# Set attention and a tanh-residual MLP on one core: weights decoded on VectorE alone, another split of the product's read-out, whole rows of natural x, a wider row pitch and a new written order

## The chip, the cores and the metric

One core of one Trainium2 chip runs the kernel. The metric is the device time of one execution in microseconds (us). The kernel before was timed in three runs: 218.50, 219.16 and 217.11 us, median 218.5. The profile shown was taken in a further execution of 216.84 us, in which the span from the first to the last instruction is 215.1 us.

## The reference

For each of 4 batches, 32 inducing vectors I attend to x (12480 rows of 128), which gives h (32 x 128); then every row of x attends to h. The result goes through an MLP without bias:

```python
def mab(q, kv):
    s = scale * (q @ kv.transpose(0, 2, 1))
    s = s - s.max(-1, keepdims=True)
    a = np.exp(s)
    a /= a.sum(-1, keepdims=True) + 1e-09
    return a @ kv
h = mab(I, x)
y = mab(x, h)
h2 = y @ w_in                       # 128 -> 2048
return ((h2 - np.tanh(h2)) @ w_out) # 2048 -> 128
```

All is fp32, except that the two weight matrices come as 64-bit floats, which the kernel turns to fp32 itself. Since y is a weighted mean of the 32 rows of h, the kernel does not run the MLP on 49920 rows: it runs a tangent form of it once per batch on the 32 rows of h ("feed", which gives a 32 x 128 table P) and then only weighs P for each row. A check at the end (lines 611 to 673) decides on the chip whether that is exact enough; the general path behind it does not run here.

## The kernel before, in words

x is cut into 4 batches of 8 steps of 1536 rows, and a remainder of 192 rows per batch. Each step's x is loaded once, transposed (channels on partitions), as a tile of 128 x 1536 (768 KB); 16 such tiles are kept. A step takes part twice.

First pass, per step: four score matmuls of x with the inducing vectors (line 311), VectorE copies them to SBUF with their running maximum (line 365). After a group of 3, 3 or 2 steps the four quarter maxima on partitions 0, 32, 64 and 96 are joined into one (lines 376 to 380), ScalarE takes the exponential of the group (line 385), VectorE transposes it in 32 x 32 blocks (line 410), and TensorE multiplies it with x in its natural layout (lines 417 and 426). Natural x comes in one of two ways: loaded from memory for 11 of 32 steps (line 392, written as 12 pieces of 512 bytes per partition, since each piece has a column of ones behind it), or by 12 transposes on TensorE, which ScalarE copies out (lines 404 and 407). When a batch's 8 steps are through, "feed" makes h and P (lines 450 to 544).

Second pass, per step: four score matmuls with the centred h (line 311 again), VectorE takes the maximum (line 552), ScalarE the exponential (554) and a weight w (556), GpSimd multiplies P with w (560), and TensorE multiplies both: 12 matmuls of 129 columns into 4 banks, the "product" (568). There is one set of 4 banks for it, so the next product waits until this one has been read. VectorE adds 1e-9 to the 12 sums and takes their reciprocals (584, 585) and scales banks 0 and 1 (588); ScalarE copies banks 2 and 3 (590), GpSimd scales these in SBUF (592); the step is then stored (603).

Each 512-column piece of a weight matrix (8 pieces) is loaded into an output tile `ot` and decoded by nine instructions on three engines: low half and mantissa on ScalarE (270, 289), bit fields on VectorE (273, 276, 284), exponent clamp, sum and scale on GpSimd (280, 281, 292, 295).

The order on every engine is that of one list: each operation has an assumed cost and a rank (a table of numbers by kind, batch and step), a list scheduler plays them through, and the instructions are issued in the order of the starts that it gives. All DMAs are issued from SyncE's queue (SP), in order: one that waits for a tile to come free holds the ones behind it.

Of the kernel before, what the change touches and what calls it, by code (L numbers as in the profile page):

```python
# [23 lines left out]
PITCH = 1536  # L24
# [5 lines left out]

POLY = (0.333333333, -0.133333309, 0.0539675967, -0.0218625754, 0.00882625035,
        -0.0034783865, 0.00124215751, -0.000337689816, 4.84671135e-05)

# [4 lines left out]

RANK = {
    "ind": [(-746.3, 138.31)],  # L40
    "load r": [(-1052.2, 40.15)],
    "r": [(-79.7, 170.53)],
    "load w": [(-698.6, 25.14)],
    "w": [(197.5, 163.77)],
    "guard": [(1549.9, 28.69)],
# [775 lines left out]
```

## Time and profile before

| what | value |
|---|---|
| median of three runs | 218.5 us (217.11 to 219.16) |
| the profiled execution: time, span | 216.84 us, 215.1 us |
| busy: TensorE, VectorE, ScalarE, GpSimd | 165.6, 155.1, 114.1, 120.3 us |
| DMA moved | 64.49 MB, 300 GB/s over the span |
| mean granted TensorE clock | 0.947 |

Busy times are sums over the whole span; no engine is busy for all of it. The DMA share of a stretch is the mean busy share of the 16 DMA engines; GB/s divided by that share is the rate while they are busy. A chain of waits lists the pieces of work that followed one another without slack, to the last instruction.

### The profile page before, as it was taken

The numbers are of one execution on the slowest core, as the hardware profiler recorded it, in microseconds if no ns is written. First come the engines' busy times: TensorE is split into PE (matmuls) and PEld (weight loads), VectorE is DVE, ScalarE is ACT, GpSimd is POOL, SyncE is SP. The second block draws the span as 40 slices with busy tenths as digits, with TensorE's granted clock in tenths as the row PEclk, the third lists the DMA queues.
The fourth block names the chain that finished last, engine by engine and source line by source line (L and its number), as shares of the span: only waits on it lengthen the run. The fifth ranks groups of instructions, "written<-read, shape, count | busy, mean of one in ns | idle before, by whom it ended". The sixth has DMA issues, their size and how long they took to land.

```text
span 215.1 us, 6700 instructions
## 1 busy us (share of the span) xinstructions
PE 165.6 (77%) x2632; PEld 103.1 (48%) x2632; DVE 155.1 (72%) x484; ACT 114.1 (53%) x223; POOL 120.3 (56%) x151
## 2 busy tenths in 40 slices
PE   2295489968799599997998799979999877634420
PEld 2163245735365276553746466546665472324310
DVE  3376979979896588895957678878679888774420
ACT  3557655758556166727537286355674535552210
POOL 2498997999204444543354166333476467877650
PEclk9999999999999999999999999999999999985555
DMA  6989975999879979999999999999455645586571
GB/s 187 365 358 365 379 274 164 348 419 420 237 249 350 362 276 384 326 397 365 374 343 348 367 332 381 356 329 351 141 218 226 252 190 240 221 330 241 207 259 66
DMA packets 27879, 64.49 MB, mean 300 GB/s; under 512 B 1504, under 2 KB 18400, under 8 KB 27840
## 3 DMA queue, kind: packets, MB, share of 16 engines
q1 hardware_dynamic: 27840, 63.99, 81.5%
q8 instruction: 23, 0.38, 0.7%
q14 instruction: 16, 0.13, 0.2%
HBM read 38.42 MB, written 25.56 MB: 298 GB/s over the span
## 4 chain that ended last, share of the span: by engine, by line
PE 31%; DMA 24%; DVE 16%; POOL 14%; issue 8%; ACT 3%; SPq 0%; POOLq 0%; ACTq 0%; DVEq 0%
DMA x<-in_xT 10%; DMA out<-ot 10%; PE PS L568 10%; PE PS L311 9%; POOL ot L280 7%; DVE ot L588 4%; PE PS L404 4%; PE PS L417 4%; DMA ot<-in_w_in 3%; POOL ot L592 3%; DVE ot L284 2%; ACT ot L590 2%; POOL ot L281 2%; POOL win_sb L292 1%; PE PS L524 1%
## 5 line engine op out<-in xcount | busy, mean ns | idle before, releaser
L592 POOL TENSOR_TENSOR ot<-ot,r 128x384 f32<-128x384 f32 (+1 forms) x66 | 53.1, 821 | 52.8 <-ACT ot L590 29.4
L407 ACT COPY xn<-PS 128x512 f32<-128x512 f32 x63 | 35.1, 587 | 18.6 <-PE PS L404 16.5
L568 PE MATMUL PS<-pw,e 32*128 32x129 f32 (+1 forms) x784 | 33.9, 304 | 13.6 <-DVE ot L588 10.9
L404 PE MATMUL PS<-ident,x 128*128 128x128 f32 x252 | 39.2, 290 | 5.5 <-DVE s L365 5.5
L568 PEld LDWEIGHTS PS<-pw,e 32*128 32x128 f32 (+1 forms) x784 | 27.5, 200 | 27.3 <-POOL ot L592 12.6
L590 ACT COPY ot<-PS 128x768 f32<-128x768 f32 (+1 forms) x33 | 26.0, 789 | 27.0 <-DMA out<-ot 11.3
L404 PEld LDWEIGHTS PS<-ident,x 128*128 128x128 f32 x252 | 27.9, 145 | 24.3 <-DVE s L365 7.2
L311 PE MATMUL PS<-x,ind_sb 128*32 128x384 f32 x256 | 27.4, 506 | 9.1 <-DMA x<-in_xT 6.3
L588 DVE TENSOR_TENSOR ot<-PS,r 128x768 f32<-128x768 f32 (+1 forms) x33 | 31.2, 945 | 3.5 <-DMA out<-ot 2.7
L560 POOL TENSOR_SCALAR pw<-P,w 128x129 f32<-128x129 f32 (+1 forms) x36 | 21.9, 612 | 17.2 <-ACT P L530 5.1
L311 PE MATMUL PS<-x,hC 128*32 128x384 f32 x256 | 26.4, 494 | 3.8 <-ACT e L554 2.3
L554 ACT ACTIVATE e<-PS,negm 128x384 f32<-128x384 f32 (+1 forms) x33 | 19.0, 577 | 17.8 <-PE PS L568 8.9
L417 PE MATMUL PS<-xn,et 128*32 128x129 f32 x672 | 24.1, 276 | 0.0
L280 POOL TENSOR_SCALAR ot<-ot 128x512 uint32<-128x512 uint32 x8 | 16.7, 2084 | 8.2 <-DVE ot L276 7.4
L417 PEld LDWEIGHTS PS<-xn,et 128*32 128x32 f32 x672 | 17.5, 109 | 5.9 <-issue 5.2
L365 DVE TENSOR_SCALAR_CACHE_REDUCE s<-PS 128x384 f32<-128x384 f32 x32 | 17.3, 548 | 4.1 <-PE PS L311 3.9
L552 DVE TENSOR_REDUCE negm<-PS 128x1 f32<-128x384 f32 (+1 forms) x33 | 17.7, 543 | 3.5 <-PE PS L311 3.3
L584 DVE TENSOR_SCALAR r<-PS 128x12 f32<-128x12 f32 (+1 forms) x33 | 5.6, 170 | 20.2 <-PE PS L568 14.4
L284 DVE SCALAR_TENSOR_TENSOR ot<-ot 128x512 uint32<-128x512 uint32 x8 | 12.9, 1612 | 7.1 <-POOL ot L281 7.0
L385 ACT ACTIVATE s<-s,nb 128x1152 f32<-128x1152 f32 (+1 forms) x12 | 13.8, 1152 | 7.3 <-DVE nb L380 7.2
L410 DVE STREAM_TRANSPOSE et<-s 128x384 f32<-128x384 f32 x32 | 16.9, 553 | 0.9 <-ACT xn L407 0.4
L311 PEld LDWEIGHTS PS<-x,ind_sb 128*32 128x32 f32 x256 | 6.0, 109 | 15.7 <-issue 5.1
(121 smaller groups left out, 183.7 us busy)
## 6 DMA issues: line engine op xcount, KB each, us to landing
x<-in_xT SPq DMA_DIRECT2D x32, 768.0 KB, 7.7
out<-ot SPq DMA_DIRECT2D x32, 768.0 KB, 4.8
xn<-in_xn SPq DMA_DIRECT2D x11, 768.0 KB, 7.5
ot<-in_w_in SPq DMA_DIRECT2D x4, 512.0 KB, 7.7
ot<-in_w_out SPq DMA_DIRECT2D x4, 512.0 KB, 4.0
xR<-in_xR SPq DMA_DIRECT2D x1, 384.0 KB, 3.0
outR<-ot SPq DMA_DIRECT2D x1, 384.0 KB, 5.0
ind_sb<-in_indT SPq DMA_DIRECT2D x1, 16.0 KB, 2.8
```

The costliest lines, as they stand in the source:

```text
L280: nc.gpsimd.tensor_scalar(out=e(), in0=e(), scalar1=896.0, scalar2=1151.0, op0=ALU.max, op1=ALU.min)
L311: nc.tensor.matmul(ps[q * m:(q + 1) * m, :n], lhsT=w(q) if callable(w) else w, rhs=row, start=True, stop=True)
L404: nc.tensor.transpose(out=ps.get()[:, j * 128:(j + 1) * 128], in_=x.get()[:, (4 * h + j) * 128:(4 * h + j + 1) * 128], identity=ident)
L407: add("ACT", 0.68, lambda ps=ps, xn=xn, h=h: nc.scalar.copy(out=xn.get()[:, 4 * h:4 * h + 4, 0:128], in_=ps.get().rearrange("p (j c) -> p ...
L417: nc.tensor.matmul(hacc.get()[q * m:(q + 1) * m, g * 130:g * 130 + 129], lhsT=et.get()[:, j, :], rhs=xn.get()[:, j, 0:129], start=(k == 0 ...
L552: add("DVE", 0.1 + T / 850, lambda: nc.vector.tensor_reduce(out=mcol, in_=ps.get()[:, :T], axis=AX.X, op=ALU.max, negate=True), reads=[ps] ...
L554: add("ACT", 0.2 + T / 1300, lambda: nc.scalar.activation(out=e2.get()[:, :T], in_=ps.get()[:, :T], func=AF.Exp, bias=mcol), reads=[ps, st ...
L560: nc.gpsimd.tensor_scalar(out=pw.get()[p, 0:129], in0=t[p, 0:129], scalar1=w.t[p], scalar2=None, op0=ALU.mult)
L568: nc.tensor.matmul(o.get()[:BL, q, k * 129:(k + 1) * 129], lhsT=e2.get()[p, k * BL:(k + 1) * BL], rhs=pw.get()[p, 0:129], start=True, stop ...
L588: add("DVE", 0.1 + 2 * T / 870, lambda: nc.vector.tensor_tensor(out=res(0, 2), in0=ov(0, 2)[:, :, :, :128], in1=wide(0, 2), op=ALU.mult), ...
L590: add("ACT", 0.2 + 2 * T / 1300, lambda: nc.scalar.copy(out=res(2, 4), in_=ov(2, 4)[:, :, :, :128]), reads=[o, ot], writes=[c], pri=("o", ...
L592: add("POOL", 0.1 + T / 500, lambda q=q: nc.gpsimd.tensor_tensor(out=res(q, q + 1).rearrange("p q k c -> p (q k) c"), in0=res(q, q + 1).re ...
```

## The change

Seven parts come together.

1. **Weights.** The nine instructions of a piece become seven on VectorE, four with one input and three with two; ScalarE and GpSimd have none. The pieces are loaded into x tiles and no longer into output tiles.
2. **Product's read-out.** VectorE takes the reciprocals of its own two banks' sums (6 per partition) straight from PSUM, ScalarE copies the sums of its two banks to SBUF, where VectorE takes their reciprocals later. The 1e-9 is put into P's column of ones. P times w moves from GpSimd to ScalarE.
3. **Last batch.** Steps 1, 3, 5 and 7 of the last batch write their product into a second set of four banks (those of the other PSUM tiles); its exponentials and outputs go into tiles that are done with.
4. **Group maxima.** The quarters are brought together by 4 GpSimd copies, one VectorE reduction, and 4 copies back, in place of 8 VectorE reductions.
5. **Natural x.** 13 steps, not 11, are loaded, as whole rows of 6336 bytes with the ones in them.
6. **Row pitch** of xT and out: 1696 in place of 1536 elements; 1536 of them are moved.
7. **Order.** The scheduler and its ranks give way to a fixed list of operation numbers. Some small matmuls of "feed" are cut into 32-column pieces, and small operations of its check move to ScalarE and GpSimd.

```diff
-PITCH = 1536
+PITCH = 1696
+ORDER = [int(n) for n in """
+1 2 3 69 0 77 4 73 21 70 74 80 75 72 71 92 76 22 94 23 83 78 95 24 93 25 90 81 26 91 29 27 82 28 37 84 79 101 85 117
...
-            buf = at("ot")
+            buf = at("x")
...
-            add("ACT", 0.7, low, reads=[buf], writes=[outs[k], lo_b], pri=p)
-            add("DVE", 0.65, bits, reads=[buf], writes=[lo_b], pri=p)
-            add("ACT", 0.65, mantissa, reads=[buf], writes=[lo_b], pri=p)
-            add("DVE", 0.65, shift, reads=[buf], writes=[e_b], pri=p)
-            add("POOL", 1.4, clamp, reads=[buf], writes=[e_b], pri=p)
-            add("DVE", 0.9, sign, reads=[buf], writes=[e_b], pri=p)
-            add("POOL", 1.4, join, reads=[buf, lo_b], writes=[outs[k]], pri=p)
-            add("POOL", 1.4, scale, reads=[buf, e_b], writes=[outs[k]], pri=p)
+            add("DVE", 0.34, magnitude, writes=[buf], pri=p, lock=True)
+            add("DVE", 0.3, clamp, writes=[buf], pri=p, lock=True)
+            add("DVE", 0.3, fields, writes=[buf], pri=p, lock=True)
+            add("DVE", 0.6, high, writes=[buf, outs[k]], pri=p, lock=True)
+            add("DVE", 0.3, power, reads=[outs[k]], writes=[buf], pri=p, lock=True)
+            add("DVE", 0.6, low, writes=[buf], pri=p, lock=True)
+            add("DVE", 0.6, join, reads=[buf], writes=[outs[k]], pri=p, lock=True)
...
+                for q in range(NQ):
+                    nc.gpsimd.tensor_copy(mq.t[:, q, :], mx.t[q * m:(q + 1) * m, :nm])
...
-        add("POOL", 0.35 * len(P4s), weigh, reads=[w, *(P4_b if len(P4s) > 1 else [P4_b[n // NS]])], writes=[pw], pri=("s2", b, s))
-        o = at("o")
+        add("ACT", 0.29, lambda: nc.scalar.activation(out=pw.get()[:, 0:129], in_=P4s, func=AF.Copy, scale=w.get()),
+            reads=[w, P_b], writes=[pw], pri=("s2", b, s))
+        o = at("o2" if last and s in SECOND else "o")
...
-            nc.vector.tensor_scalar(out=rs.t[:BL], in0=ov(0, NQ)[:, :, :, 128], scalar1=1e-9, scalar2=None, op0=ALU.add)
-            nc.vector.reciprocal(out=rs.t[:BL], in_=rs.t[:BL])
+        add("DVE", 0.05 + 0.016 * nv * nb, lambda: recip(*sums(0, nv)), reads=[o, rs], writes=[ra], pri=("o", b, s))
+        add("ACT", 0.1, lambda: nc.scalar.copy(out=sums(nv, NQ)[1], in_=sums(nv, NQ)[0]), reads=[o, rs], writes=[rc], pri=("o", b, s))
...
-        "xn": np.ascontiguousarray(np.stack([xs[b, s].reshape(KB, 128, C).transpose(1, 0, 2) for b, s in sorted(LOADED)])),
+        "xn": np.stack([np.pad(xs[b, s].reshape(KB, 128, C).transpose(1, 0, 2), ((0, 0), (0, 0), (0, 4)), constant_values=1.0)
+                        for b, s in sorted(LOADED)]),
```

Three places show how the instructions move. GpSimd's queue at the start, behind its memsets (`ot` an output tile with a raw weight piece, `mx` the maxima of a group, `nb` their joined negative). Before:

```order
L280 TENSOR_SCALAR ot_100<-ot_100 128x512
L281 TENSOR_SCALAR ot_100<-ot_100 128x512
L280 TENSOR_SCALAR ot_101<-ot_101 128x512
L281 TENSOR_SCALAR ot_101<-ot_101 128x512
L292 TENSOR_TENSOR win_sb<-win_sb,ot_100 128x512
L295 TENSOR_TENSOR win_sb<-win_sb,ot_100 128x512
```

In the change:

```order
L378 COPY mq_0_131<-mx_129 32x4 x4
L385 COPY nb_130<-nq_0_132 32x1 x4
L378 COPY mq_1_135<-mx_1_134 32x3 x4
L385 COPY nb_130<-nq_1_136 32x1 x4
L378 COPY mq_2_138<-mx_2_137 32x2 x4
L385 COPY nb_130<-nq_2_139 32x1 x4
```

All 32 weight instructions leave this queue, and the copies of the group maxima enter it.

SP's queue at the start, from its third DMA. Before:

```order
L267 DMA ot_100<-in_w_in 128x1024
L267 DMA ot_101<-in_w_in 128x1024
L355 DMA x_80<-in_xT 128x1536
L267 DMA ot_102<-in_w_in 128x1024
L355 DMA x_81<-in_xT 128x1536
L267 DMA ot_103<-in_w_in 128x1024
L355 DMA x_82<-in_xT 128x1536
L267 DMA ot_100<-in_w_out 128x1024
```

In the change:

```order
L357 DMA x_81<-in_xT 128x1536
L275 DMA x_82<-in_w_in 128x1024
L357 DMA x_83<-in_xT 128x1536
L357 DMA x_84<-in_xT 128x1536
L275 DMA x_85<-in_w_in 128x1024
L275 DMA x_86<-in_w_out 128x1024
L357 DMA x_87<-in_xT 128x1536
```

The fifth piece had to wait for the decoding of the first, in `ot_100`; now the eight pieces are spread over six x tiles, and only the last two, further down, wait for the decoding of another.

TensorE's queue at the end, the products of the last batch (`pw` is P times w; `e`, or `s` and `xn` tiles used again, hold the exponentials). Before:

```order
L568 MATMUL PS<-pw_112,e_109 128x129 x12
L311 MATMUL PS<-x_89,hC 32x384 x4
L568 MATMUL PS<-pw_114,e_111 128x129 x12
L311 MATMUL PS<-x_88,hC 32x384 x4
L568 MATMUL PS<-pw_113,e_110 128x129 x12
L311 MATMUL PS<-xR,hC 32x192 x4
L568 MATMUL PS<-pw_112,e_109 128x129 x12
```

In the change:

```order
L313 MATMUL PS<-x_85,hC 32x384 x4
L587 MATMUL PS<-pw_114,s_105 128x129 x12
L657 MATMUL PS<-fold,cs 128x8
L313 MATMUL PS<-xR,hC 32x192 x4
L587 MATMUL PS<-pw_115,s_105 128x129 x12
L587 MATMUL PS<-pw_114,s_106 128x129 x12
L587 MATMUL PS<-pw_116,s_105 128x129 x12
L587 MATMUL PS<-pw_115,s_106 128x129 x12
```

The last batch's scores are all ahead of its second product, and the products then follow one another. Between the last matmul of the first pass and the end, TensorE had 13 full products and that of the remainder; it has 14 and that of the remainder now. SP's queue has 17 full stores behind its last load, where it had 16.

## Rows read from the trace of the kernel before

**Rows 1.** The page: the span; busy time, share of the span and instructions of four engines; the granted clock in 40 equal slices, in tenths of full speed.

```profile
span 215.1 us, 6700 instructions
PE 165.6 (77%) x2632; PEld 103.1 (48%) x2632; DVE 155.1 (72%) x484; ACT 114.1 (53%) x223; POOL 120.3 (56%) x151
...
PEclk9999999999999999999999999999999999985555
```

**Rows 2.** Stretches of the span (us from its start): length, busy time of each engine (instructions), granted clock (1.00 is 2.4 GHz), DMA share, GB/s.

```profile
2.60:155.00 152.40, 129.36 (x1998) 79.99 (x1998) 117.57 (x375) 88.26 (x169) 81.51 (x86) 1.00 0.94 335
...
25.00:40.00 15.00, 12.25 (x172) 7.60 (x172) 13.36 (x33) 10.06 (x19) 13.66 (x11) 1.00 0.75 250
...
45.00:50.00 5.00, 3.60 (x70) 2.15 (x63) 4.44 (x10) 2.74 (x5) 4.83 (x5) 1.00 1.02 420
...
60.00:65.00 5.00, 5.00 (x110) 3.17 (x102) 4.47 (x21) 2.51 (x6) 0.18 (x1) 1.00 0.76 236
...
130.00:136.00 6.00, 6.00 (x84) 3.73 (x84) 5.27 (x17) 3.62 (x7) 3.60 (x6) 1.00 1.01 375
...
155.00:208.00 53.00, 36.25 (x646) 23.15 (x634) 36.28 (x103) 24.58 (x55) 37.00 (x53) 0.85 0.58 234
...
175.00:190.00 15.00, 11.08 (x210) 6.31 (x202) 11.33 (x32) 8.32 (x22) 12.18 (x17) 1.00 0.62 251
190.00:208.00 18.00, 7.37 (x113) 5.98 (x112) 8.86 (x24) 5.22 (x9) 12.04 (x17) 0.56 0.62 249
```

**Rows 3.** What SP's queue waited for: us in total, times, longest.

```profile
SPq L603 <- DVE ot L588: 49.2, 28, 5.1
SPq L603 <- POOL ot L592: 37.3, 29, 2.9
...
SPq L267 <- POOL win_sb L292: 18.0, 4, 5.2
```

**Rows 4.** SP's issues in order of time: start us, us to the end of the last, what, count; then, from the page, the remainder's store: count, KB, median us from issue to landing.

```profile
60.68 0.55 SPq L392 DMA_DIRECT2D xn<-in_xn  x1
...
115.75 0.55 SPq L392 DMA_DIRECT2D xn<-in_xn  x1
...
136.79 4.15 SPq L392 DMA_DIRECT2D xn<-in_xn  x2
...
148.32 0.55 SPq L392 DMA_DIRECT2D xn<-in_xn  x1
155.96 50.28 SPq L603 DMA_DIRECT2D out<-ot  x16
208.24 0.35 SPq L611 DMA_DIRECT2D outR<-ot  x1
...
outR<-ot SPq DMA_DIRECT2D x1, 384.0 KB, 5.0
```

**Rows 5.** The chain of waits, in order of time: start, us, what. First the end of the last batch's first pass, then one turn from product to product, then the last product.

```profile
161.80 0.37 DVE hsb L456
...
180.12 0.99 PE PS L568 x24
...
185.36 0.98 PE PS L568 x24
186.44 0.18 DVE r L584
186.65 0.24 DVE r L585
186.91 0.97 DVE ot L588
188.02 0.98 PE PS L568 x24
...
200.24 0.97 DVE ot L588
201.35 1.71 PE PS L568 x24
...
204.72 1.32 PE PS L568 x16
```

**Rows 6.** The weights' lines: duration in ns, minimum, median and maximum, first and last start; and one group of GpSimd's by busy us and mean ns.

```profile
L284 DVE SCALAR_TENSOR_TENSOR ot<-ot x8: 693/1757/1778, 10.6 to 52.5; 128x512 uint32<-128x512 uint32 x8
...
L276 DVE TENSOR_SCALAR ot<-ot x8: 407/417/1454, 7.4 to 42.5; 128x512 uint32<-128x512 uint32 x8
...
L280 POOL TENSOR_SCALAR ot<-ot 128x512 uint32<-128x512 uint32 x8 | 16.7, 2084 | 8.2 <-DVE ot L276 7.4 <-DVE nbm L450 0.4
```

**Rows 7.** Groups of one form: busy us, mean ns | idle us before them and what ended it.

```profile
L590 ACT COPY ot<-PS 128x768 f32<-128x768 f32 x32 | 25.4, 795 | 24.8 <-DMA out<-ot 11.3 <-DVE r L584 8.4 <-PE PS L568 2.4
...
L554 ACT ACTIVATE e<-PS,negm 128x384 f32<-128x384 f32 x32 | 18.6, 582 | 14.8 <-DVE negm L552 8.7 <-PE PS L568 6.0
...
L380 DVE TENSOR_REDUCE nb<-mq 32x1 f32<-32x4 f32 x48 | 7.1, 147 | 0.9
L556 ACT ACTIVATE w<-negm 128x1 f32<-128x1 f32 x33 | 6.5, 201 | 3.8 <-DVE negm L552 3.8
...
L436 ACT ACTIVATE s1R<-s1R,nb 128x64 f32<-128x64 f32 x4 | 1.4, 350 | 0.0
...
L518 POOL COPY us<-g 128x16 f32<-128x16 f32 x4 | 0.8, 212 | 7.5 <-DVE gp L499 4.5 <-DVE g L515 3.1
```

More of the change, by code (lines that the diff above doesn't have):

```diff
@@ new lines, in behind @@
+    def behind(self, tag, tags):
+        before = {op for op in self.ops if any(x.tag in tags for x in op.bufs)}
+        for op in self.ops:
+            if any(x.tag == tag for x in op.bufs):
+                op.deps |= before - {op}
+    def order(self):
+        free = {tag: [(0.0, t) for t in tiles] for tag, tiles in self.places.items()}
+        avail, mode, locked = {"SP": 2.6}, None, 0.0
+        ops = [self.ops[n] for n in ORDER]
+        for op in ops:
+            start = max([avail.get(op.eng, 0.0), *(d.end for d in op.deps)])
+            for x in op.bufs:
+                if x.tag and x.t is None:
+                    free[x.tag].sort(key=lambda f: f[0])
+                    since, x.t = free[x.tag].pop(0)
+                    start = max(start, since)
+            cost = op.cost
+            if op.mode:
+                cost += SWITCH.get(op.mode, 0.1) * (op.mode != mode)
+                mode = op.mode
+            if op.lock:
+                start = max(start, locked)
+                locked = start + cost
+            op.start = start
+            avail[op.eng] = start + cost
+            op.end = start + cost + op.lag
+            for x in op.bufs:
+                x.left -= 1
+                x.since = max(x.since, op.end)
+                if x.tag and not x.left:
+                    free[x.tag].append((x.since, x.t))
+        self.span = max(op.end for op in ops)
+        return ops
@@ L549, in tail, with res_of @@
+        add("POOL", 0.6, terms, reads=[hi, y, cols0_b], writes=[h2, absm, colp_b[b]], pri=("f", b, 20))
+    def res_of(ot):
+        t = ot.get()
+        return t if len(t.shape) == 3 else t.rearrange("p (j d) -> p j d", d=128)
+    def tail(n, ps, T, BL, P4s, P_b, b, s, store):
         nb = T // BL
-        e2, pw, w, rs = at("e2"), at("pw"), small(f"w{n}", [128, 1]), small(f"r{n}", [128, NQ, nb])
+        last = b == B - 1
+        e2, pw, w, rs = at("e2t" if last else "e2"), at("pw"), at("w"), at("r")
@@ L590, in tail, with sums @@
-        add("ACT", 0.2 + 2 * T / 1300, lambda: nc.scalar.copy(out=res(2, 4), in_=ov(2, 4)[:, :, :, :128]), reads=[o, ot], writes=[c], pri=("o", b, s))
-        for q in (2, 3):
-            add("POOL", 0.1 + T / 500, lambda q=q: nc.gpsimd.tensor_tensor(
+            return rs.get()[:BL, q0:q1, :nb].unsqueeze(3).to_broadcast([BL, q1 - q0, nb, 128])
+        nv = SHARE[b]
+        ra, rc, a, c = (Buf() for _ in range(4))
+        def sums(q0, q1):
+            return ov(q0, q1)[:, :, :, 128], rs.get()[:BL, q0:q1, :nb]
@@ L593, in tail @@
+        add("ACT", 0.12 + (NQ - nv) * T / 1340, lambda: nc.scalar.copy(out=res(nv, NQ), in_=ov(nv, NQ)[:, :, :, :128]),
+            reads=[o, ot], writes=[c], pri=("o", b, s))
+        add("DVE", 0.05 + 0.016 * (NQ - nv) * nb, lambda: recip(sums(nv, NQ)[1], sums(nv, NQ)[1]), reads=[rs], writes=[rc], pri=("o", b, s + 0.5))
+        for q in range(nv, NQ):
+            add("POOL", 0.05 + T / 520, lambda q=q: nc.gpsimd.tensor_tensor(
                 out=res(q, q + 1).rearrange("p q k c -> p (q k) c"), in0=res(q, q + 1).rearrange("p q k c -> p (q k) c"),
@@ L602, in second @@
-        tail(b * NS + s, ps, SEG, 128, [(slice(0, 128), P4[:, b, :])], b, s,
-             lambda t: nc.sync.dma_start(out=out[b, s], in_=t.rearrange("p j d -> p (j d)")))
+        add("PE", 0.66, lambda: scores(ps.get(), hC[:, b, :], [x.get()[:, q * SEG:(q + 1) * SEG] for q in range(NQ)]),
+            mode="C", reads=[x, hC_b[b]], writes=[ps], pri=("s2", b, s))
+        tail(b * NS + s, ps, SEG, 128, P4[:, b, 0:129], P4_b[b], b, s,
+             lambda t: nc.sync.dma_start(out=out[b, s, :, :SG], in_=t.rearrange("p j d -> p (j d)")))
```

357 lines of the change are left out of this document (148 added, 209 removed), and 41 rows, old and new, of tables (ORDER, RANK).

## The prediction

> **What bounds the kernel now.** I read the page first, then stretches of the span, then SP's queue, then the chain of waits. The page shows no engine busy for more than 77% of the 215.1 us [rows 1], so the sums alone name no bound; the stretches do. From 2.6 to 155 us the DMA share is 0.94 at 335 GB/s, while TensorE is busy for 129.36 of 152.4 us. From 155 to 208 us the share is 0.58 at 234 GB/s [rows 2]. So the reader sees two kernels: a front bound by transfers, and a tail of 16 stores that arrives at the rate at which results are made.
>
> In the front the engines of the DMA move 335/0.94 = 356 GB/s while busy. Without a natural-x load in flight, from 130 to 136 us, between those issued at 115.75 and 136.79 [rows 4], it is 375/1.01 = 371. From 60 to 65, right behind one issued at 60.68, it is 236/0.76 = 310. From 45 to 50 us, loads of x almost alone, it is 420/1.02 = 412 [rows 2]. The largest hole is from 25 to 40 us, share 0.75, and SP's queue says why: it waited 18.0 us for GpSimd's weight decoding before it could load the next piece, with loads of x behind it [rows 2, 3].
>
> In the tail the chain of waits goes round one loop: product 0.98, add 0.18, reciprocal 0.24, scaling of two banks 0.97, and the next product starts 2.66 us after the one before (185.36 to 188.02); later, at the lower clock, 3.37 (201.35 to 204.72) [rows 5]. There is one set of product banks. Stores wait for VectorE's and GpSimd's half of it, 49.2 and 37.3 us in all [rows 3].
>
> **The change, term by term.** The sum is made against the profiled execution: 216.84 us, 1.7 more than its span; the median of the runs is 0.8% above it, and I leave the forecast at the profiled level.
>
> *Bytes of the front.* To the last load, SP's new queue moves 32 x of 0.786 MB, 13 natural x of 0.811, 8 weight pieces of 0.524, 0.4 of small loads and 15 stores: 25.2 + 10.5 + 4.2 + 0.4 + 11.8 = 52.1 MB, 1.0 more than the 335 x 152.4 = 51.1 MB of before.
>
> *Rate.* Whole rows of 6336 bytes should move as other rows do; the bounds are 310 (no gain over the stretch with 512-byte pieces) and 412 GB/s. I take 371, the row with loads and stores together: 140.4 us busy. The Trainium skill (DMA: Bandwidth & Descriptors, Specifications) puts line rate at 512 bytes and up, by which whole rows gain nothing: the rate would stay 356, the front would take 6 us longer, and the sum would be 199. The trace speaks against it, with 310 beside 371 [rows 2].
>
> *Holes.* At share 0.94 the front loses 9.1 of 152.4 us; 3.75 of these are the hole at 25 to 40, which the new staging removes, since only the last two weight pieces wait for a decoding. That leaves 0.965: 140.4/0.965 = 145.5, and with the first 2.6 us the last load has landed at **148.1**. TensorE does not bind there: 129.36 us and the 6.8 to 161.8 make 136.2, with the start 138.8 at most, and two steps' transposes fall away.
>
> *VectorE in the front.* 117.57 us before [rows 2]. It takes on 8 pieces of three two-input instructions at 0.693, the shortest of line 284, and four others at 0.417: 30.0 us. The upper end is the median of line 284, 1.757, beside GpSimd's clamps of 2.084 [rows 6]; GpSimd has only short copies left then, so I take the lower. It loses line 284's eight (14 us at the median) and the 48 reductions of line 380 (7.1) [rows 7]. About 126 of 145.5 us: hidden, but with little to spare.
>
> *ScalarE.* P times w costs between 0.2 (one element, line 556) and 0.582 (384 elements); I take line 436's 0.350. The copy of the sums I put at 0.2. Per step that makes 0.582 + 0.201 + 0.350 + 0.2 + 0.795 = 2.13 us [rows 7]. In the front, 88.26 us [rows 2] and 18 steps of 0.55 more: hidden.
>
> *GpSimd* loses the clamps (16.7 of line 280 alone) and P times w; hidden.
>
> *Tail, first part.* From the last first-pass product to the last batch's first own product took 161.80 to 180.12 = 18.3 us with five products in between [rows 5]. Now it is six. The new loop has no add (0.21 with its gap) and half the reciprocal: 2.66 - 0.21 - 0.05 = 2.4. Six of them are 14.4, which lies above what "feed" itself needs; the other end is 18.3. With one step's matmuls of about 1.0 in front: 148.1 + 1.0 + 14.4 = 163.5.
>
> *Tail, second part.* Eight products on two sets of banks. The loop now spans two steps, so 2.4 no longer binds, nor does the product at the lower clock (1.71). What does is ScalarE's 2.13 a step, and the store: 0.786 MB at 371 GB/s is 2.12. 8 x 2.13 = 17.0, to 180.5. Here the second set saves 0.53 a step against 2.66, and 1.24 against 3.37.
>
> *The clock.* It was granted 1.00 from 175 to 190 us with TensorE busy for 11.08 of 15, and fell to 0.56 on average from 190 to 208 with 7.37 of 18 [rows 2]: from 2.4 towards 1.2 GHz once the scores had run out. The new queue has the scores ahead of the products, so I expect the fall again, at about 0.98/2.13 busy, at no cost but in the last product.
>
> *The end.* From the remainder's product to the end of the span: 204.72 to 215.1 = 10.4 us [rows 1, 5], of which its store's landing is 5.0 [rows 4]. It is kept.
>
> Sum: 148.1 + 1.0 + 14.4 + 17.0 + 10.4 = 190.9 us span, **192.6 us** as a time. The 17 stores and the remainder's, 13.8 MB at 371, need 37 us from 148.1, to 185.3: just inside, so stores are the second bound of the tail. The pitch I put at nothing: the rows stay contiguous for 6144 bytes.
>
> **Rivals.** Faster than that: the rate goes to the 412 of x alone. The front would be 52.1/0.412/0.965 + 2.6 = 133.6, so that TensorE's 138.8 binds: 138.8 + 1.0 + 14.4 + 17.0 + 10.4 + 1.7 = 183. Against it, the stretch that mixes loads and stores shows 371. Chance 0.13.
>
> A smaller gain. (a) The maxima's way. Eight reductions of 0.147 become eight copies of 0.212, a reduction, and two hand-overs between engines: 0.7 us more before a group's exponential, and every matmul of the group stands behind that. If each copy is held for one two-input VectorE instruction, 8 x 0.693 = 5.5 us more per group, 33 us over the six groups beside the weights; half of it covered, the time is 209. The Trainium skill (SBUF — State Buffer, Who interferes with whom) says that such VectorE instructions and GpSimd's reads exclude each other, so its rule is on this rival's side; line 284's 693 and 1757 ns agree. (b) The new order fits the chip no better than the old: 356 GB/s at 0.94 gives 158.3 for the front, then 1.0 + 18.3 + 8 x 2.66 + 10.4 + 1.7 = 211. Together 0.23.
>
> No change, 216 to 220.7: (b) with a little more. 0.05.
>
> Slower: **the wider pitch** slows x and the stores. All 64 row transfers, 50.3 MB, now lie 6784 bytes apart, where they were one contiguous block a tile. At 371 GB/s they are 135.6 us of the sum. Nothing in the trace shows another pitch; the nearest slow row is 310, which gives 162.3 and a time of 219.3. It decides from 307 GB/s down: at 300 the time is 224.7. Against it, one row is one piece of 6144 bytes as before. Chance 0.09.
>
> **How the numbers follow.** The forecast has 0.50, with its own range from 186 to 200. The range takes in the faster rival and most of the smaller gain and leaves out about 0.2: 180 to 207. About 1% is what a measurement of this kernel can tell from no change (its three runs spread over 0.9%). Faster by over 1%: 0.13 + 0.50 + 0.23 = 0.86; within it 0.05; slower 0.09.
>
> **What would show it.** In the profile after: SP's queue no longer waits for weights; share 0.96 or more up to the last load, at about 371 GB/s while busy; the last load landed near 148 us; VectorE's two-input weight instructions near 0.69 us, GpSimd under 100 us busy; products of the last batch 2.1 us apart with the clock low at the end. I am wrong if the loads of x move below 350 GB/s, if the first three groups' exponentials come more than 2 us behind their maxima, or if the last batch's first own product is more than 18 us behind the first pass.

## The result, and the profile after

The changed kernel takes 197.0 us, median of four runs (195.42 to 198.23), beside 217.8 us (216.34 to 219.16) for the kernel before on the same chip: a ratio of 0.904, 95% interval 0.894 to 0.914. Forecast were 192.6 us, with a range of 180 to 207. The profiled execution took 197.96 us; its span is 196.1. Some executions of most kernels below run slower, mostly at a lower granted clock, and medians and ratios leave these out.

First the page, with the rows that answer to [rows 1], the DMA share and the GB/s of each slice.

```profile
span 196.1 us, 6902 instructions
...
PE 156.4 (80%) x2776; PEld 101.9 (52%) x2776; DVE 136.9 (70%) x392; ACT 113.5 (58%) x283; POOL 83.8 (43%) x197
...
PEclk9999879999999999999999996999999999996755
DMA  5999999609999999999999999899997646888891
GB/s 166 360 419 420 412 415 389 238 7 342 401 382 413 411 346 372 399 366 414 362 398 368 411 399 351 283 343 362 425 417 290 264 165 258 333 351 360 329 362 43
```

GpSimd fell from 120.3 to 83.8 us, VectorE from 155.1 to 136.9. The DMA row has one new thing: the slices with 6 and 0, at 34 to 44 us. The stretches, with the columns of [rows 2]:

```profile
2.60:147.00 144.40, 127.90 (x2180) 82.85 (x2180) 104.68 (x297) 84.31 (x200) 54.06 (x140) 0.98 0.95 365
...
34.00:44.00 10.00, 8.96 (x172) 6.92 (x174) 8.65 (x22) 5.54 (x11) 4.01 (x8) 1.00 0.37 130
...
148.96:167.63 18.67, 16.79 (x352) 9.73 (x344) 15.25 (x42) 14.00 (x43) 11.12 (x21) 1.00 0.59 235
167.63:182.50 14.87, 10.15 (x212) 8.21 (x212) 11.10 (x34) 10.43 (x32) 10.62 (x14) 0.89 0.88 354
182.50:196.10 13.60, 0.53 (x20) 0.31 (x13) 3.94 (x13) 1.48 (x5) 4.96 (x7) 0.55 0.64 231
```

The cuts of the last three are read from TensorE's rows (start, us, what, count; in brackets what it waited for): the last first-pass matmuls, the first of the last batch's products, and the row that holds its eighth (24 matmuls) and the remainder's (16).

```profile
148.09 0.87 PE L422 MATMUL PS<-xn,et 128*32 128x129 f32 x24 [0.95 <-DMA xn<-in_xn]
...
167.63 0.95 PE L587 MATMUL PS<-pw,s 32*128 32x129 f32 x24
...
169.86 0.95 PE L587 MATMUL PS<-pw,s 32*128 32x129 f32 x24 [0.49 <-DVE x L613]
171.66 0.95 PE L587 MATMUL PS<-pw,s 32*128 32x129 f32 x24 [0.85 <-ACT pw L579]
172.83 0.95 PE L587 MATMUL PS<-pw,s 32*128 32x129 f32 x24 [0.21 <-DVE x L613]
...
181.64 1.39 PE L587 MATMUL PS<-pw,xn 32*128 32x129 f32 x40 [1.37 <-ACT pw L579]
```

Set beside the forecast's terms, in us:

| part | forecast | measured | difference |
|---|---|---|---|
| start to the end of the first pass | 149.1 | 148.96 | -0.1 |
| to the first of the last batch's products | 14.4 | 18.67 | +4.3 |
| eight products, to the remainder's | 17.0 | 14.87 | -2.1 |
| to the end of the span | 10.4 | 13.60 | +3.2 |
| span | 190.9 | 196.1 | +5.2 |

SP's waits, as [rows 3], and its issues around the new hole and at the end, as [rows 4]:

```profile
SPq L630 <- POOL ot L619: 38.3, 20, 3.6
SPq L357 <- PE PS L313: 32.4, 13, 5.2
SPq L357 <- DVE win_sb L299: 11.0, 2, 9.8
...
SPq L357 <- DVE wout_sb L299: 8.1, 1, 8.1
```

```profile
18.07 25.39 SPq L357 DMA_DIRECT2D x<-in_xT  x6
...
139.89 0.38 SPq L397 DMA_DIRECT2D xn<-in_xn  x1
...
188.02 0.35 SPq L638 DMA_DIRECT2D outR<-x  x1
```

Before, pieces of weights waited for GpSimd's decoding, 18.0 us. Now loads of x (L357) wait for VectorE's, 11.0 + 8.1 us: six loads took from 18.07 to 43.46 us to be issued, because x tiles that they needed held raw weights. That is the hole at 34 to 44, 10 x 0.63 = 6.3 us of transfers.

### The profile page after: what moved, and what is told of

It reads as the page before. It is cut to its first block, busy times and chain, and to the rows that moved or that the text cites. A ratio compares the mean times of both kernels' runs of the same rounds, so it can differ in the third digit from the quotient of the medians.

```text
span 196.1 us, 6902 instructions
## 1 busy us (share of the span) xinstructions
PE 156.4 (80%) x2776; PEld 101.9 (52%) x2776; DVE 136.9 (70%) x392; ACT 113.5 (58%) x283; POOL 83.8 (43%) x197
## 5 line engine op out<-in xcount | busy, mean ns | idle before, releaser
L619 POOL TENSOR_TENSOR ot<-ot,r 128x384 f32<-128x384 f32 x48 | 39.1, 829 | 35.5 <-DVE r L610 9.3
L378 POOL COPY mq<-mx 32x4 f32<-32x4 f32 (+2 forms) x48 | 10.0, 209 | 48.8 <-DVE s L367 47.2
L587 PE MATMUL PS<-pw,e 32*128 32x129 f32 x576 | 24.0, 294 | 2.6 <-DVE ot L613 1.3
L613 DVE TENSOR_TENSOR ot<-PS,r 128x768 f32<-128x768 f32 x24 | 22.8, 950 | 4.2 <-DMA out<-ot 3.8
L587 PEld LDWEIGHTS PS<-pw,e 32*128 32x128 f32 x576 | 19.2, 191 | 10.6 <-DVE ot L613 3.4
L615 ACT COPY ot<-PS 128x768 f32<-128x768 f32 x24 | 19.3, 805 | 8.9 <-PE PS L587 4.6
L422 PEld LDWEIGHTS PS<-xn,et 128*32 128x32 f32 x672 | 18.6, 110 | 9.6 <-issue 5.2
L385 POOL COPY nb<-nq 32x1 f32<-32x1 f32 x48 | 14.5, 302 | 11.1 <-DVE nq L380 9.6
L619 POOL TENSOR_TENSOR x<-x,r 128x384 f32<-128x384 f32 (+1 forms) x18 | 14.0, 805 | 4.7 <-DVE r L610 1.5
L575 ACT ACTIVATE e<-PS,negm 128x384 f32<-128x384 f32 x24 | 13.6, 585 | 4.2 <-DVE negm L573 3.9
L579 ACT ACTIVATE pw<-P,w 128x129 f32<-128x129 f32 x32 | 12.7, 413 | 0.1
```

The costliest lines, as they stand in the source:

```text
L385: nc.gpsimd.tensor_copy(nbs.t[q * m:(q + 1) * m, g:g + 1], nq.t)
L422: nc.tensor.matmul(hacc.get()[q * m:(q + 1) * m, g * 130:g * 130 + 129], lhsT=et.get()[:, j, :], rhs=xn.get()[:, j, 0:129], start=(k == 0 ...
L587: nc.tensor.matmul(o.get()[:BL, q, k * 129:(k + 1) * 129], lhsT=e2.get()[p, k * BL:(k + 1) * BL], rhs=pw.get()[p, 0:129], start=True, stop ...
L613: add("DVE", 0.06 + nv * T / 960, lambda: nc.vector.tensor_tensor(out=res(0, nv), in0=ov(0, nv)[:, :, :, :128], in1=wide(0, nv), op=ALU.mult),
L615: add("ACT", 0.12 + (NQ - nv) * T / 1340, lambda: nc.scalar.copy(out=res(nv, NQ), in_=ov(nv, NQ)[:, :, :, :128]), reads=[o, ot], writes=[c ...
L619: add("POOL", 0.05 + T / 520, lambda q=q: nc.gpsimd.tensor_tensor(out=res(q, q + 1).rearrange("p q k c -> p (q k) c"), in0=res(q, q + 1).r ...
```

## The experiments

Twelve kernels were run, on several chips; beside them the kernel before had medians of 216.2 to 217.2 us (217.8 beside the changed kernel), so a difference of 2 us between two medians is not told from nothing. The ratios are to the kernel before on the same chip. Three runs have too few executions counted for one.

| run | what is altered | median us, executions counted (range of all) | ratio to before, 95% |
|---|---|---|---|
| changed kernel | | 197.0, 4 of 4 (195.4 to 198.2) | 0.904 [0.894, 0.914] |
| 1 | pitch 1536 | 196.8, 6 of 6 (196.3 to 199.1) | 0.915 [0.908, 0.922] |
| 2 | natural x in pieces | 198.9, 2 of 4 (197.7 to 202.9) | |
| 3 | one set of banks | 206.8, 3 of 5 (205.7 to 210.4) | 0.956 [0.946, 0.967] |
| 4 | maxima on VectorE | 199.0, 3 of 4 (196.8 to 201.5) | 0.920 [0.910, 0.929] |
| 5 | before, new weights | 217.0, 9 of 10 (215.3 to 218.8) | 0.999 [0.995, 1.003] |
| 6 | before, whole rows | 215.3, 3 of 4 (214.6 to 222.2) | 0.988 [0.980, 0.995] |
| 7 | weights staged in `ot` | 196.4, 4 of 4 (194.6 to 197.5) | 0.904 [0.898, 0.910] |
| 8 | one read-out first | 194.6, 1 of 6 (194.6 to 204.2) | |
| 9 | old weights | 213.6, 4 of 5 (213.2 to 216.7) | 0.987 [0.980, 0.995] |
| 10 | old sums | 199.6, 2 of 4 (198.4 to 204.4) | |
| 11 | feed stretch reordered | 196.6, 3 of 6 (195.5 to 202.2) | 0.910 [0.901, 0.918] |
| 12 | 7, and reordered again | 198.4, 4 of 6 (196.1 to 201.0) | 0.920 [0.914, 0.925] |

**1, the pitch.**

```diff
-PITCH = 1696
+PITCH = 1536
```

> The changed kernel with rows of x and of the output 6144 bytes apart again, as before, and nothing else altered. My theory (the pitch costs and brings nothing): 195.5 to 198.5 us, ratio to the kernel before the same 0.90, stretch 60 to 90 us again at about 385 GB/s, landing of x about 8.1 us. Rival 1 (the wider pitch slows row transfers, and eats a part of the gain): below 195, the first pass ends before 147 us. Rival 2 (the wider pitch is where the faster front comes from): above 200, and the stretch 60 to 90 falls back towards 371 GB/s or below.

The same time by the medians; the ratios' intervals overlap, so an effect of 1 or 2% is not excluded. From 2.6 to 147 us the transfers ran at 366 GB/s, share 0.95, with the old pitch, and at 365 and 0.95 with the wide one. (From 60 to 90 us they are 406 and 385 GB/s, from 90 to 120 us 373 and 391.) The pitch neither slows the rows nor carries the bulk of the gain.

**2 and 6, whole rows undone, and alone.**

```diff
-nc.sync.dma_start(out=xn.get(), in_=xnat(b, s))
+nc.sync.dma_start(out=xn.get()[:, :, 0:128], in_=xnat(b, s))
```

> The changed kernel with natural x loaded into 512-byte pieces again (128 of each 132 words of a row), same order, same thirteen loads. Theory (whole rows save transfer time and the front is bound by transfers): before, the stretch with such a load moved 310 GB/s at a share of 0.76 over 5 us where 371 was usual, which is 0.6 us a load; thirteen of them 8 us, so the first pass ends at 153 to 157 us instead of 149, and the time is 201 to 205 us. Rival (pieces of 512 bytes already move as whole rows do, or TensorE, busy for 127.9 of 144.4 us, binds the front): first pass at 149 to 150 us, time 196 to 198.5.

> The kernel before with its eleven loads of natural x in whole rows of 6336 bytes and nothing else altered; every engine's order is the old one. Theory (0.3 to 0.6 us of transfers saved a load, as the reverse run's 3.4 us for thirteen loads and my estimate of 0.6 bound it): 3 to 6 us less, 211 to 214. Rival (the loads are covered, or 512-byte pieces already move at full rate): 216 to 218.

In run 2, 1.9 us lost for 13 loads, by two executions, which alone show nothing. In run 6, 1.2% = 2.7 us won for 11 by the ratio (1.9 by the medians): 0.2 us a load, where I had worked out 0.6 from the one stretch at 310 GB/s [rows 2]. By the rate while busy the transfers themselves did gain about that much. The front of run 6:

```profile
2.60:155.00 152.40, 131.80 (x1974) 81.14 (x1974) 117.03 (x375) 88.32 (x167) 81.01 (x85) 0.98 0.91 337
```

While busy, the DMA engines moved 337/0.91 = 370 GB/s, and 335/0.94 = 356 without whole rows [rows 2]. In run 2 they moved 361/0.99 = 365 from 2.6 to 147 us, and 365/0.95 = 384 in the changed kernel. Over the bytes of these fronts that is an estimated 5 and 7 us of transfers, about 0.5 us a load (no more than an estimate: the share is not exact, it reads 1.07 from 60 to 90 us in run 2). But the share fell as the rate rose: what the rows save became in large part idle time of the DMA engines.

**3, one set of banks.**

```diff
-SECOND = (1, 3, 5, 7)
+SECOND = ()
```

> The changed kernel without the second set of product banks in the last batch; the order of every engine is the same but for three read-outs. Theory as predicted (a loop of 2.3 to 2.66 us a step instead of the products' present spacing): the products from 167.6 to about 182 us (14 us) take 8 x 2.4 = 19 us, and the remainder's store is issued 3 to 5 us later: 200 to 202 us. Rival 1 (the stores bind the tail, share 0.90 at 358 GB/s from 170 to 188): the products come later but the last store does not, 196.5 to 198.5. Rival 2 (the low clock makes the loop 3.37 as before): 205 us.

9.8 us slower, the largest loss but one. The last batch's products, and the stretch that holds them (of an execution of 210.32 us, 3.6 above the median; the mean granted clock was 0.909 in it and 0.909 to 0.911 in the three counted, against 0.943 to 0.961 in the changed kernel):

```profile
176.47 0.95 PE L610 MATMUL PS<-pw,s 32*128 32x129 f32 x24 [2.11 <-DVE x L636]
178.69 1.68 PE L610 MATMUL PS<-pw,s 32*128 32x129 f32 x24 [1.27 <-DVE x L636]
182.01 1.67 PE L610 MATMUL PS<-pw,s 32*128 32x129 f32 x24 [1.65 <-DVE x L636]
...
196.50 1.19 PE L610 MATMUL PS<-pw,xn 32*96 32x129 f32 x16 [1.70 <-DVE x L636]
```

```profile
171.00:197.00 26.00, 13.27 (x216) 10.31 (x216) 12.95 (x40) 11.48 (x34) 12.60 (x17) 0.62 0.61 244
```

With one set TensorE waits for each read-out, the granted clock falls at the fourth product (0.62 over the stretch), a product then takes 1.67 us and not 0.95, and the loop grows to 3.3 us and more. From 171.19 to 196.50 us the eight intervals took 25.3 us; with two sets 14.9. Eight times the price at the low clock (1.24 a step in the prediction, [rows 5]) is 9.9 us, which is what was lost; eight times 0.53 would be 4.2.

**4, group maxima on VectorE.**

```diff
-nc.gpsimd.tensor_copy(mq.t[:, q, :], mx.t[q * m:(q + 1) * m, :nm])
+nc.vector.tensor_copy(mq.t[:, q, :], mx.t[q * m:(q + 1) * m, :nm])
```

(and the four copies back in the same way)

> The changed kernel with the eight small copies of each group's maxima made by VectorE instead of GpSimd, in the same places of the order. Theory (the hand-over between engines is covered by other work in the front): 195.5 to 198.5 us. Rival (a) of the prediction (each group's exponential waits 2 us and more for GpSimd's copies, and the matmuls behind it too): the time falls to 190 to 195, and the idle time of ScalarE in front of the exponential goes. Rival the other way (VectorE, which holds x tiles until the weights are decoded, is the scarce engine between 20 and 45 us): 199 or more, with the transfers' hole longer than 34 to 44 us.

Not faster; 2.0 us slower by the medians, with overlapping intervals. The hand-over that rival (a) feared is there, though. In the changed kernel, GpSimd's copies and ScalarE's exponential for the second group, beside the weights, and the fourth, when only the last instruction of the sixth piece ran beside the copies:

```profile
28.05 1.33 POOL L378 COPY mq<-mx 32x3 f32<-32x3 f32 x4 [7.35 <-DVE s L367]
29.79 2.19 POOL L385 COPY nb<-nq 32x1 f32<-32x1 f32 x4 [0.42 <-DVE nq L380]
...
45.57 0.85 POOL L378 COPY mq<-mx 32x4 f32<-32x4 f32 x4 [5.74 <-DVE s L367]
46.68 1.25 POOL L385 COPY nb<-nq 32x1 f32<-32x1 f32 x4 [0.26 <-DVE nq L380]
```

```profile
32.01 1.26 ACT L390 ACTIVATE s<-s,nb 128x1152 f32<-128x1152 f32 x1 [0.97 <-POOL nb L385]
...
47.96 0.35 ACT L441 ACTIVATE s1R<-s1R,nb 128x64 f32<-128x64 f32 x1 [0.98 <-POOL nb L385]
```

From the first copy to the exponential 4.0 us beside the weights, 2.4 in the fourth group; in the first and third it was 4.7 and 4.5. On VectorE the second group's way took 3.1 us (26.27 to 29.36), 0.9 less, and the time was no better. Either the wait is covered, or VectorE, busy for 117.6 us up to 147 in place of 104.7, lost elsewhere what it saved there: the run does not tell these apart.

**5, the new weights alone, in the kernel before.** Apart from the weights, every engine's order is the old one, row for row; the three instructions that stood for GpSimd's `scale` follow one another.

```diff
-            add("DVE", 0.65, shift, reads=[buf], writes=[e_b], pri=p)
+            add("DVE", 0.65, magnitude, reads=[buf], writes=[e_b], pri=p)
...
-            add("DVE", 0.9, sign, reads=[buf], writes=[e_b], pri=p)
+            add("DVE", 0.9, lambda fields=fields, high=high: (fields(), high()), reads=[buf], writes=[e_b], pri=p)
...
-            add("POOL", 1.4, scale, reads=[buf, e_b], writes=[outs[k]], pri=p)
+            add("POOL", 1.4, lambda power=power, low=low, join=join: (power(), low(), join()), reads=[buf, e_b], writes=[outs[k]], pri=p)
```

> The kernel before with the weights decoded by VectorE alone in the seven new instructions, staged in the output tiles as before; the order of TensorE and of the transfers is the old one, row for row. Theory (the change's first part removes the 18.0 us wait of SP's queue and with it the hole from 25 to 40 us, 3.75 us of transfers, but no more): 212 to 215 us, against 216 to 218 for before. Rival 1 (the weights on GpSimd were what the whole front waited for): below 210. Rival 2 (30 us of VectorE in place of 14 on VectorE delay the first pass): 218 or more.

No change to 0.5%. The wait of SP's queue only changed its name, from GpSimd's 18.0 us to VectorE's:

```profile
SPq L270 <- DVE ot L291: 19.2, 4, 7.6
```

**9, the old weights, in the changed kernel.** The nine old instructions stand in the places of the seven, in the tiles of x.

```diff
-            add("DVE", 0.34, magnitude, writes=[buf], pri=p, lock=True)
+            add("DVE", 0.34, lambda low=low, bits=bits: (low(), bits()), writes=[buf], pri=p, lock=True)
...
-            add("DVE", 0.6, join, reads=[buf], writes=[outs[k]], pri=p, lock=True)
+            add("DVE", 0.6, scale, reads=[buf], writes=[outs[k]], pri=p, lock=True)
```

> The changed kernel with the old decoding of the weights on ScalarE, VectorE and GpSimd, in the places of the order that the new one has, staged in tiles of x as now. The weights alone changed nothing in the kernel before (ratio 0.9989), where the wait for GpSimd became a wait for VectorE of 19.2 us. Theory (there another cover hid it, here loads of x wait for these tiles): the hole in the transfers, 34 to 44 us now, begins as early and ends 3 to 8 us later, the first pass ends at 151 to 156, 200 to 205 us. Rival (the weights' path is covered in both kernels, TensorE and the bytes bind): 196 to 198.5.

16.6 us slower by the medians, twice the most that I had expected. Stretches (of an execution of 216.65 us, 3.1 above the median), then SP's issues and its two waits for weights:

```profile
34.00:44.00 10.00, 4.74 (x59) 2.71 (x57) 2.42 (x8) 4.97 (x9) 7.78 (x12) 0.93 0.01 3
44.00:57.00 13.00, 11.64 (x172) 9.12 (x176) 8.03 (x17) 7.49 (x14) 11.59 (x16) 0.79 0.37 124
```

```profile
17.85 39.08 SPq L361 DMA_DIRECT2D x<-in_xT  x6
```

```profile
SPq L361 <- POOL wout_sb L303: 25.2, 3, 17.2
SPq L361 <- POOL win_sb L303: 11.2, 2, 8.7
```

The six loads of x now took 39 us to be issued, the hole grew from 6.3 to 10 x 0.99 + 13 x 0.63 = 18.1 us, TensorE ran dry (4.74 of 10 us) and its clock fell (0.79 from 44 to 57), and the first pass ended at 167.46 us, 18.5 later: all of the hole came through, and more. Run 5 and this one change the same decoding: worth nothing in one order, 16.6 us in the other. But run 5 stages the pieces in output tiles and this one in tiles of x, and the new order was written for one engine's decoding; how much of the 16.6 is staging and misfit was not run.

**7, the weights staged in the output tiles.**

```diff
-            buf = at("x")
+            buf = at("ot")
```

> The changed kernel with the weight pieces staged in the four output tiles instead of tiles of x; same order but for which tile is taken. Theory (the transfers' hole from 34 to 44 us, 6 us of them, comes from six tiles of x held until VectorE has decoded the pieces, and the front is bound by transfers): SP's queue no longer waits 25.4 us on six loads of x at 18 to 43 us, the last first-pass matmuls come at 142 to 146 instead of 148.1, time 191 to 195. Rival (TensorE, busy 8.96 of 10 us in the hole and 127.9 of 144.4 in the front, binds as well, so the transfers only idle elsewhere): 196 to 198.5, with share 0.95 or less again up to the last load.

The hole is gone (first row: share 0.98 where it was 0.37), and the first pass ends at 146.0 us in place of 149.0. These are single executions, but run 12, staged in the same way, has 145.3, and no profile of the changed kernel with staging in tiles of x has less than 148.1. Half of the 6.3 us came through to there, and of the time, by the medians, no more than 0.6 us, which this measurement cannot tell from nothing.

```profile
34.00:44.00 10.00, 8.96 (x155) 6.66 (x153) 8.37 (x22) 5.03 (x10) 3.81 (x8) 1.00 0.98 380
2.60:145.00 142.40, 125.11 (x2180) 81.22 (x2180) 105.17 (x298) 85.56 (x203) 55.04 (x141) 0.99 0.98 375
```

```profile
SPq L420 <- PE PS L445: 18.6, 4, 8.9
```

Loads of natural x now wait 18.6 us for TensorE to be done with their tiles. TensorE was busy for 8.96 of the 10 us of the hole in the changed kernel too: once the transfers run ahead, they wait for TensorE.

**10, the old sums.**

```diff
+        def old_sums():
+            src, dst = sums(0, NQ)
+            nc.vector.tensor_scalar(out=dst, in0=src, scalar1=0.0, scalar2=None, op0=ALU.add)
+            nc.vector.reciprocal(out=dst, in_=dst)
-        add("DVE", 0.05 + 0.016 * nv * nb, lambda: recip(*sums(0, nv)), reads=[o, rs], writes=[ra], pri=("o", b, s))
+        add("DVE", 0.05 + 0.016 * nv * nb, old_sums, reads=[o, rs], writes=[ra], pri=("o", b, s))
-        add("ACT", 0.1, lambda: nc.scalar.copy(out=sums(nv, NQ)[1], in_=sums(nv, NQ)[0]), reads=[o, rs], writes=[rc], pri=("o", b, s))
+        add("ACT", 0.1, lambda: None, reads=[o, rs], writes=[rc], pri=("o", b, s))
```

(the second reciprocal of line 617 goes too; the add has 0, and P's column of ones keeps the 1e-9)

> The changed kernel with the old read-out's sums: VectorE adds and takes the reciprocals for all twelve sums, ScalarE copies none. Two sets of banks as now. Theory (the loop on one set grows from 2.31 to about 2.5 us, by the 0.2 of the add, six times between the first pass and the last batch, and VectorE's 0.2 a step hides on two sets): 0.8 to 1.5 us longer in that stretch, 197 to 199.5. Rival (the sums' copy on ScalarE costs as much as it saves): 196 to 197. Rival the other way (VectorE and ScalarE are full in the last 15 us, and each add shows): 200 to 202.

2.6 us slower, but by two executions (198.35 and 200.90, beside 195.42 to 198.23): unclear. What the profile shows is the loop: turns with nothing of feed's in between took 2.57 to 2.66 us (149.98 to 152.64, 164.74 to 167.31, 167.31 to 169.91) in place of 2.3.

**8, 11 and 12, the stretch between the first pass and the last batch.** In the changed kernel the six products there start at 149.53, 151.85, 155.51, 160.26, 163.02 and 165.33. Undisturbed turns take 2.3 us; the two of 3.66 and 4.75 stand behind small operations of feed. Run 8 moved one read-out forward (VectorE's queue; ScalarE's half likewise, and the next product on TensorE):

```diff
 TENSOR_REDUCE hi<-PS
+RECIPROCAL r<-PS
+TENSOR_TENSOR ot<-PS,r
 TENSOR_TENSOR us<-PS,gp
...
-RECIPROCAL r<-PS
-TENSOR_TENSOR ot<-PS,r
```

> The changed kernel with one product's read-out, of the six between the first pass and the last batch's own products, put ahead of the feed's row products in the queues of VectorE and ScalarE, and the next product one place earlier on TensorE. Theory (the 4.2 us that this stretch took over six loops of 2.3 come from read-outs that stand behind the feed's small operations in in-order queues): that product's successor starts 1 to 2 us earlier (3.2 us after it instead of 4.75), the first of the last batch's products 0.8 to 1.6 us earlier relative to the end of the first pass (17.0 to 17.8 instead of 18.6 us), time 195 to 197. Rival (the feed's own chain, 14.9 us to its last copy, binds, and is now delayed by 0.6 us): 18.6 us or more.

Its executions scatter over 10 us, so I read only that TensorE stood inside the moved product, waiting for ScalarE's half. Run 11 moved both halves and more; on TensorE:

```diff
 MATMUL PS<-pw,e
+MATMUL PS<-pw,e
 MATMUL PS<-x,hC
 MATMUL PS<-x,hC
 MATMUL PS<-wout_sb,us
 MATMUL PS<-pw,e
-MATMUL PS<-x,hC
-MATMUL PS<-ot,cols
 MATMUL PS<-p,F
-MATMUL PS<-pw,e
+MATMUL PS<-x,cols
+MATMUL PS<-ot,cols
+MATMUL PS<-x,hC
```

> The changed kernel with the feed stretch of the last but one batch reordered as a whole: the third product's read-out ahead of the feed's row product on VectorE and ahead of the square on ScalarE, the fourth and fifth products two and five places earlier on TensorE, the guard's sixteen matmuls and three scores behind them, one of the guard's two staging tiles taken from x. The run before moved VectorE's half alone; ScalarE's copy then waited behind an operation that waits for VectorE, TensorE stood inside the product for 1.13 us, and the stretch grew. Theory (the stretch is six loops of 2.31 plus what the queues' order puts in between, 4.2 us): 2 us of it go, first product of the last batch 16.2 to 17.2 us after the first pass in place of 18.6, time 195 to 196.5. Rival (TensorE, busy for 17.6 of the 20 us, binds, and the moved scores only come back as waits later): 18 us or more, 197 or more.

Run 12 also staged the weights as in run 7 and put the guard's matmuls (`cols`) behind the sixth product.

> The changed kernel with the weights staged in the output tiles as in the seventh run, and the stretch between the first pass and the last batch ordered once more: as in the eleventh run, but with both of the guard's staging tiles in tiles of x and its sixteen matmuls behind the sixth product, so that nothing on TensorE waits for GpSimd's terms (1.45 us of waiting in that run) and four output tiles are free all the way. Theory (what the eleventh run moved came back as the guard's wait): first pass at 145 to 147, the first of the last batch's products 16 to 17.8 us behind it, 192.5 to 195. Rival (that stretch is full on several engines at once, and each order gives the same 18.6 us or more): 195.5 to 198, like the seventh run or a little more.

Not faster, and run 12 is slower than run 7 (ratios 0.920 and 0.904, intervals apart). The rows of run 12:

```profile
144.47 0.87 PE L444 MATMUL PS<-xn,et 128*32 128x129 f32 x24 [1.28 <-DMA xn<-in_xn]
...
154.12 1.35 PE L609 MATMUL PS<-pw,e 32*128 32x129 f32 x24 [1.28 <-DVE ot L635]
...
157.70 0.95 PE L609 MATMUL PS<-pw,e 32*128 32x129 f32 x24
...
161.79 0.95 PE L609 MATMUL PS<-pw,e 32*128 32x129 f32 x24
...
163.34 1.06 PE L675 MATMUL PS<-x,cols 128*32 128x128 f32 x32
...
166.52 0.95 PE L609 MATMUL PS<-pw,s 32*128 32x129 f32 x24
```

```profile
145.34:166.52 21.18, 17.54 (x352) 9.85 (x345) 15.67 (x42) 15.44 (x43) 12.18 (x22) 1.00 0.58 233
```

The fourth and fifth products came 2.5 and 1.7 us earlier after the first pass, the sixth did not (161.79 - 145.34 = 16.45 us after it; 165.33 - 148.96 = 16.37 before the move), and the first of the last batch's came 21.2 us after it in place of 18.7. What I took out of one place came back in another, in run 11 as well (21.3 us). The rival fits: TensorE has about 17 us of its own work in this stretch, and the rest is waits that move about. About 7.5 of the 17 are ten steps' scores, which the order puts there; no run moved them behind the mark, where TensorE had time.

## Why the forecast was right, and where not

The sign and the size come from where the prediction put them: a shorter front by fuller transfers, and a last batch that no longer waits for one set of banks. Of the 19.0 us by which the span is shorter, the front up to the end of the first pass gives 12.8 (161.80 before) and the eight products 9.7 (180.12 to 204.72 = 24.6 before) [rows 5]; the two other parts take back 0.4 and 3.2. Run 3 shows the banks behind the 9.7. The 12.8 no run gives to one part.

**The front** came out at 148.96 us against 149.1, which is luck: two errors cancel. The rate while busy was 365/0.95 = 384 GB/s, above the 371 that I took and within its bounds; the share was 0.95 and not 0.965. That whole rows raise the rate was right (356 to 370 in run 6, where nothing else changed); the rest, to 384, came with the new order, and no run explains it. The step "the hole at 25 to 40, which the new staging removes, since only the last two weight pieces wait for a decoding" failed: the pieces no longer wait, but the loads of x do, in the same queue, for the same decoding. I had looked at what the moved loads wait for, and not at who waits for the tiles that they take. Run 7 shows that only about 3 us of the new hole reach the end of the first pass, because TensorE then holds the queue.

**VectorE in the front**: forecast about 126 us, measured 104.7. The instructions have their forecast length:

```profile
L278 DVE TENSOR_SCALAR x<-x 128x512 uint32<-128x512 uint32 x8 | 3.3, 420 | 4.6 <-DMA x<-in_w_in 3.2 <-DMA x<-in_w_out 1.4
...
L289 DVE SCALAR_TENSOR_TENSOR win_sb<-x 128x512 uint32<-128x512 uint32 x4 | 2.7, 663 | 0.0
...
L579 ACT ACTIVATE pw<-P,w 128x129 f32<-128x129 f32 x32 | 12.7, 413 | 0.1
```

What I forgot is that the old decoding's sixteen one-input instructions go as well, and so do the adds (2.9 us in the front before). In the kernel before:

```profile
L273 DVE TENSOR_SCALAR ot<-ot 128x512 uint32<-128x512 uint32 x8 | 6.3, 791 | 0.1
...
L276 DVE TENSOR_SCALAR ot<-ot 128x512 uint32<-128x512 uint32 x8 | 4.5, 567 | 4.1 <-DMA ot<-in_w_in 4.1
```

That is 10.8 us. And of the maxima's 96 reductions I took off line 380's 48 alone; line 378's 48, another 6.7 us, go too, and 12 new ones cost 1.7. The reciprocals gained nothing: split in two, they took 6.2 us up to 147 us and 3.9 up to 155 us before. The error cost nothing that the runs show.

**Tail, first part** is the term that was mis-sized: "Six of them are 14.4, which lies above what feed itself needs". The turn of 2.4 us was right (2.3). But I summed the loop and feed's chain, and never TensorE's own work between the two marks: ten steps' scores, six products and feed's and the guard's matmuls, 16.79 of the 18.67 us at full clock. The trace of the kernel before had said so; the same stretch there:

```profile
161.80:180.12 18.32, 15.76 (x273) 8.97 (x265) 15.87 (x54) 9.12 (x23) 10.63 (x16) 1.00 0.57 227
```

15.8 of 18.3 us, with one product fewer. The other end that I named, 18.3, was the right one, and by the prediction's own mark (more than 18 us) this step was wrong.

**Tail, second part**: 14.87 us against 17.0. ScalarE's step was 2.18 us where I had 2.13 (0.585 + 0.208 + 0.413 + 0.171 + 0.80), but six of the eight exponentials were done or begun before the first product; the products came 1.2 to 3.3 us apart, 2.0 on average from 167.63 to 181.64. The clock did fall, to 0.89 on average over these 15 us.

**The end**: 13.60 us against 10.4. I kept the old tail of a loop in which GpSimd was done with one product before the next came. Now the eighth product and the remainder's come right behind one another, and GpSimd's last six scalings stand in one row of 4.32 us (start, us, what). So the remainder's store was issued 5.5 us after its product began (188.02), where it had been 3.5 (208.24 behind 204.72, [rows 4, 5]): 2.0 of the 3.2 us. The profile's chain of what ended last goes through these scalings too. The stores, the second bound that the prediction named, came close: share 0.97 from 185 to 190 us, and the remainder's landed 5.5 us after its issue (5.0 in [rows 4]). The two last parts together are 28.5 us, and 27.4 were forecast.

```profile
183.67 4.32 POOL L619 TENSOR_TENSOR x<-x,r 128x384 f32<-128x384 f32 x6 [0.53 <-ACT r L612]
```

**The rivals.** The slower one, the pitch, fell by run 1. Of the smaller gain, (a)'s delay is real: the first three groups' exponentials came 4.0 to 4.7 us behind their maxima, where the prediction had put more than 2 us as a sign of being wrong. That sign came true and the time did not follow it; the delay was 1.5 to 2.2 us more than in the fourth group, not the 5.5 of the rival, and no run shows it in the time (run 4). What stays open: the parts do not add up. Undone one at a time, the two whose loss is clear, weights 16.6 and banks 9.8, lose 26.4 us of a gain of 20.8 (sums 2.6, rows 1.9 and maxima, moved to VectorE, 2.0 are too near to what cannot be told), and the weights alone bring nothing. How much is the new order's own was not run, nor the two further loads of natural x alone.

## What to carry to other kernels

When a change shortens a loop inside a stretch, sum each engine's own work between the two marks, not only the loop and the longest chain: the next bound is already in the trace of before. When a load moves to other tiles, ask who waits for these tiles; the wait goes with the work. And a part is not worth one number: undo it in the new kernel and put it alone into the old one, since the same decoding was worth 0 us in one order and staging and 16.6 in another.

## What the runs showed of the hardware

GpSimd's small copies stretched beside VectorE's two-input instructions on the weights: four copies of 32 x 1 took 2.66, 2.19 and 3.14 us in the first three groups, 1.25 in the fourth, beside one such instruction, and 0.84 in the fifth, beside none, while VectorE's own stayed at 663 ns on average. The Trainium skill (SBUF — State Buffer, Who interferes with whom) has a VectorE instruction with two SBUF inputs and a GpSimd instruction that reads SBUF shut each other out of a shared pair of ports; the trace agrees, and here the engine with the short operations paid.

Rows 6784 bytes apart moved as rows 6144 bytes apart do (365 and 366 GB/s at a share of 0.95 up to 147 us). Natural x as whole rows of 6336 bytes took about 0.5 us less of transfer a load than as pieces of 512 bytes, an estimate from the rates of runs 2 and 6 (365 to 384 and 356 to 370 GB/s while busy). And TensorE's clock made a saved wait worth about twice its price: the set of banks that I had priced at 0.53 us a step, from turns at 2.4 GHz, saved 9.8 us over eight, because with one set waits of 2.11 and 1.27 us came first, the granted clock then fell (0.62 on average from 171 to 197 us), and each product took 1.67 us in place of 0.95. That the waits caused the fall is the order of events; no run had one set and a clock that stayed up.
